# Mixture-of-experts units sized by an ordering of the experts, with 32-token runs computed from the arriving weights

## The chip, the core and the metric

The kernel runs on one core of one Trainium2 chip. The metric is the device time of one execution in microseconds (us), as a median over runs. TensorE is called PE here, VectorE DVE, ScalarE ACT, GpSimd POOL and SyncE SP, as the profile does.

## The reference

Three layers follow each other on 2304 tokens of width 512.

```python
def _attn_ref(q, k, v):                      # (4, 8, 576, 64)
    ...                                      # block-causal attention, blocks of 64
def _moe_ref(x, w_in, w_out):                # 512 -> 2048 -> 512
    h = x @ w_in
    return (h - np.tanh(h)) @ w_out
def _moe2_ref(x, w_skip, w_gate, w1, w2):    # 8 experts, 512 -> 1024 -> 512
    do_compute = x @ w_skip > 0
    out = x.copy()
    xc = x[do_compute]
    e_idx = np.argmax(xc @ w_gate, axis=1)
    gate_w = ...                             # softmax of the logits, at e_idx
    for e in range(8):
        mask = e_idx == e
        y[mask] = gate_w[mask, None] * (np.maximum(xc[mask] @ w1[e], 0.0) @ w2[e])
    out[do_compute] = xc + y
    return out
```

So in the third layer each token that passes the skip gate goes through one expert. With the reference's inputs 1264 of the 2304 tokens do, and experts 0 to 7 get 269, 0, 3, 130, 211, 176, 406 and 69 of them.

## The kernel before, in words

Attention comes first, then the first feed-forward layer (`moe1`, in groups of 384 tokens), then the experts (`Moe2`). The change is in the last part.

While `moe1` finishes a group, it computes that group's gate and scatters for each token a record (row number, gate weight) into the DRAM table `tab` (L685). Each expert has a region of `tab`; unused rows hold a row number past the last token, for which the gather reads zeros and the scatter writes nothing. After four of the six groups, `Route.pick` names the expert with most tokens so far the **lead** (expert 6 here), whose weights are loaded before `moe1` ends. `Route.close` leaves room so that the lead's first 256 rows belong to the first five groups and can be used before the last group is routed.

The experts are computed in **units** of 256 or 128 tokens of one expert. `Moe2.run` walks through **steps** s. A unit of 256 has 8 steps: step z multiplies one 128-wide slice of the hidden layer, `mm1` (L834: 12 matmuls of 256 columns, since each factor is split in a high and a low part), and two steps later `mm2` for that slice (L893: 6 matmuls of 512 columns). A unit of 128 has 4 steps with `mm1_few` (L846, 12 of 256 columns), two transposes (L860) and `mm2_few` (L874, 6 of 512 columns). Before, the units are two of 256 for the lead and seven more from `UNITS` (256, 256, 128, 256, 128, 256, 128), which makes 60 steps. Which expert and rows a unit of `UNITS` gets is computed at run time by `entries` (L1030 to L1092, on DVE) and read into registers by `expert` and `first_row`; an expert of more than 256 tokens takes several units and its weights are loaded for each. If more units are needed, a loop at the end (L1253) computes them one by one; with these inputs it runs zero times.

A unit's weights are 8 pieces of 512 KB. `load_piece` (L769, L772, on SP's queue) brings one into a `stage` buffer, of which there are four; `split_piece` writes its high part (L787, on ACT) and its low part (L788, on DVE) into one of two weight sets. `todo` lists at which step each piece is split; after each split the next load is issued, so four are always on their way. At s = `THEN` the registers are read and the first four loads are issued. A unit's tokens come by `load_rec` (L792) and `gather` (L801, an indirect DMA on POOL), four transposes per 128 tokens (L812) and a split (L819, L820). `finish` (L905, L908) adds the token itself and scatters the result. All instructions stand in each engine's queue in the order in which `run` writes them.

The steps of attention that the prediction compares with are L200 (scores, a full-width fp32 matmul) and L293 (`pv_early`, fp32 matmuls whose result fills 64 of the 128 output partitions, for two heads).

## Time and profile before

| | us |
|---|---|
| median of 3 runs | 868.16 (867.09 to 871.84) |
| the profiled execution, its own time | 870.14 |
| its span, first to last instruction | 868.6 |
| PE busy | 832.7 (96%) |
| DVE busy | 698.7 (80%) |
| ACT busy | 565.6 (65%) |
| POOL busy | 249.3 (29%) |
| DMA, mean rate | 122 GB/s |

Busy time is the time in which an engine had an instruction under way. Matmuls overlap in the pipeline, so a row's mean duration is longer than the distance from one to the next; the distance is read from starts. "Idle before" is time in which an engine had nothing under way, with what ended it behind the arrow. A row of the timeline merges equal instructions that follow each other without a gap: its start, how long the whole row took, and behind the x how many.

### The profile page before, as it was taken

To read this page: it belongs to the slowest core of one execution; us is meant where nothing else is said; L and a number is where in the kernel's file an instruction comes from. 1 tells how busy PE (TensorE), PEld (TensorE's weight loads), DVE (VectorE), ACT (ScalarE), POOL (GpSimd) and SP (SyncE) were. 2 spreads that over 40 slices of the span, in tenths; PEclk is the share of its full clock that TensorE was granted. 3 is DMA by queue.
4 is the path that set the end of the run, shared out by engine and by line. 5 is a ranking of instruction groups with operands and counts; after the bars stand their busy time and mean duration, and the time that the engine had idled before them with its cause. 6 is when DMAs were issued, how large, how long until landed. Compare 5 with 4: busy or idle time off the path is not lost.

```text
span 868.6 us, 14970 instructions
## 1 busy us (share of the span) xinstructions
PE 832.7 (96%) x4715; PEld 710.9 (82%) x4715; DVE 698.7 (80%) x1681; ACT 565.6 (65%) x1332; POOL 249.3 (29%) x314
## 2 busy tenths in 40 slices
PE   7999999999899999999999999999998889999996
PEld 4777777777787989999899898988886789999995
DVE  6899999999799999989986868777797626777772
ACT  5788888888577776776775555646565115565651
POOL 5767777677311111111100010010103221214101
PEclk9899999999999999999999999999999989999998
DMA  7356353652123332232320404222354326687850
GB/s 171 89 143 159 93 141 88 151 127 88 59 80 89 96 121 88 95 122 73 102 89 21 146 11 137 80 68 82 90 191 124 102 103 211 197 299 255 290 193 25
DMA packets 102836, 106.06 MB, mean 122 GB/s; under 512 B 64807, under 2 KB 75175, under 8 KB 102754
## 3 DMA queue, kind: packets, MB, share of 16 engines
q1 hardware_dynamic: 99554, 98.52, 37.8%
q0 software_dynamic: 3200, 6.55, 2.4%
q8 instruction: 38, 0.62, 0.3%
q14 instruction: 44, 0.36, 0.1%
HBM read 82.61 MB, written 23.78 MB: 122 GB/s over the span
## 4 chain that ended last, share of the span: by engine, by line
PE 35%; issue 34%; DVE 17%; ACT 5%; DMA 3%; POOL 3%; SPq 1%; POOLq 0%; DVEq 0%; ACTq 0%
PE h L200 6%; PE h L834 6%; PE acc L893 5%; PE h L508 4%; PE acc L561 4%; DVE w L538 3%; PE acc L266 2%; DVE st L208 2%; DVE w L542 2%; DVE word L51 2%; DVE word L52 1%; DMA xr<-x2s,rec 1%; PE lp L316 1%; PE tp L316 1%; POOL tab L685 1%
## 5 line engine op out<-in xcount | busy, mean ns | idle before, releaser
L508 PE MATMUL h<-xhl,wi 128*128 128x384 f32 x1152 | 220.4, 340 | 1.1 <-DVE xhl L449 1.1
L508 PEld LDWEIGHTS h<-xhl,wi 128*128 128x128 f32 x1152 | 204.9, 188 | 8.8 <-DVE xhl L449 1.3
L561 PE MATMUL acc<-wo,gh 128*128 128x512 f32 x576 | 151.0, 397 | 2.9 <-ACT o L578 2.9
L561 PEld LDWEIGHTS acc<-wo,gh 128*128 128x128 f32 x576 | 105.3, 188 | 21.9 <-ACT o L578 5.0
L240 POOL TENSOR_TENSOR p<-p,st 128x64 f32<-128x64 f32 (+2 forms) x144 | 103.4, 723 | 60.4 <-DVE st L239 27.6
L200 PE MATMUL h<-kT,qbd 128*128 128x128 f32 (+7 forms) x320 | 106.0, 423 | 4.6 <-ACT p L219 1.9
L536 DVE SCALAR_TENSOR_TENSOR w<-h,u 128x384 f32<-128x384 f32 x96 | 53.3, 555 | 46.4 <-ACT t L534 38.9
L561 PE MATMUL acc<-wo,gl 128*128 128x512 f32 x288 | 83.1, 397 | 2.0 <-DVE gl L550 2.0
L685 POOL DMA_INDIRECT tab<-rec,pi x18 | 20.2, 1124 | 212.4 <-DVE pi L683 198.9
L534 ACT ACTIVATE t<-h 128x384 f32<-128x384 f32 x96 | 47.1, 491 | 49.0 <-DVE w L542 49.0
L834 PE MATMUL h<-xhl,wi 128*128 128x256 f32 x576 | 78.7, 286 | 0.0
L533 ACT ACTIVATE u<-h 128x384 f32<-128x384 f32 x96 | 47.2, 492 | 48.2 <-issue 41.1
L834 PEld LDWEIGHTS h<-xhl,wi 128*128 128x128 f32 x576 | 76.0, 192 | 3.2
L893 PE MATMUL acc<-wo,hp 128*128 128x512 f32 x288 | 75.7, 399 | 0.0
L538 DVE SCALAR_TENSOR_TENSOR w<-y,w 128x384 f32<-128x384 f32 x96 | 71.6, 746 | 0.0
L219 ACT ACTIVATE p<-h,st 128x64 f32<-128x64 f32 (+7 forms) x128 | 65.0, 509 | 7.3 <-DVE st L234 5.7
L561 PEld LDWEIGHTS acc<-wo,gl 128*128 128x128 f32 x288 | 53.8, 188 | 16.3 <-DVE gl L550 3.7
L208 DVE TENSOR_REDUCE st<-h 128x1 f32<-128x64 f32 (+7 forms) x128 | 57.0, 445 | 10.3 <-PE h L200 9.5
L200 PEld LDWEIGHTS h<-kT,qbd 128*128 128x128 f32 x320 | 50.6, 196 | 15.9 <-issue 5.8
L881 ACT ACTIVATE hp<-h 128x256 fp32r<-128x256 f32 x48 | 18.4, 384 | 65.1 <-PE h L834 61.2
L542 DVE COPY_PREDICATED w<-k,t 128x384 f32<-128x384 int32 x96 | 57.3, 597 | 3.8 <-ACT k L541 3.7
L541 ACT ACTIVATE k<-u,bias 128x384 f32<-128x384 f32 x96 | 60.0, 625 | 0.0
(233 smaller groups left out, 1611.1 us busy)
## 6 DMA issues: line engine op xcount, KB each, us to landing
stage<-in_moe_w_dram SPq DMA_DIRECT2D x64, 512.0 KB, 4.5
xg<-xTd SPq DMA_DIRECT2D x48, 192.0 KB, 2.4
stage<-in_moe_w_in_dram SPq DMA_DIRECT2D x16, 512.0 KB, 3.8
stage<-in_moe_w_out_dram SPq DMA_DIRECT2D x16, 512.0 KB, 3.2
x2p<-o SPq DMA_DIRECT2D x18, 256.0 KB, 4.4
part<-x2p SPq DMA_DIRECT2D x18, 256.0 KB, 3.0
out_dram<-part SPq DMA_DIRECT2D x18, 256.0 KB, 2.3
x2s<-part SPq DMA_DIRECT2D x18, 256.0 KB, 2.9
```

What stands on the lines that cost most here:

```text
L200: nc.tensor.matmul(s[:, 0:z - a], qb[:, i, :], kT[:, a:z], start=True, stop=True)
L208: nc.vector.reduce_max(nm, ss[0][:, 0:nk], axis=AX.X, negate=True)
L219: nc.scalar.activation(prob[i][:, 0:nk], ss[0][:, 0:nk], AF.Exp, bias=nm, accum_out=st[:, 1, i:i + 1])
L240: nc.gpsimd.tensor_tensor(prob[i][:, 0:nk], prob[i][:, 0:nk], ri.to_broadcast([128, nk]), op=ALU.mult)
L508: nc.tensor.matmul(h[:, 0:TG], w[:, a, c, fs], x[:, b, c], start=(n == 0), stop=(n == 11))
L536: nc.vector.scalar_tensor_tensor(w, h, POLY_C2, u, op0=ALU.mult, op1=ALU.mult)
L538: nc.vector.scalar_tensor_tensor(w, y, POLY_K, w, op0=ALU.add, op1=ALU.mult)
L541: nc.scalar.activation(k, u, AF.Relu, bias=C.bias[:, 1:2])
L542: nc.vector.copy_predicated(w, k.bitcast(I32), t)
L561: nc.tensor.matmul(accs[u][t], g[a][:, t * 128:t * 128 + 128], w[:, b, f], start=(f == 0 and b == 1), stop=(f == NF - 1 and a == 1),)
L834: self.nc.tensor.matmul(h[:, 0:NSLOT], wi[:, a, c, f * 128:f * 128 + 128], x[:, b, c], start=(n == 0), stop=(n == 11))
L893: nc.tensor.matmul(acc[t], hp[:, a, t * 128:t * 128 + 128], wo[:, b, f], start=(f == 0 and b == 1), stop=(f == 7 and a == 1),)
```

## The change

Experts are now put into seven **slots**: slot 0 is the lead, slots 1 to 6 the others by falling token count. Each slot has a capacity, from its units and, for slots 1, 4 and 6, a run of 32 more tokens: 512, 288, 256, 256, 160, 128 and 32. The units stand fixed in the code: 256, 128 and 128 for the lead, 256 each for slots 1 to 3, 128 each for slots 4 and 5; that makes 48 steps. With these inputs every expert fits into its slot, and the loop for what is left over runs zero times again. `Route.close` now leaves 384 rows for the first five groups, so the lead's second unit is gathered early as well.

The runs of 32 tokens are computed by a new function, `few`, without splitting anything: it takes each weight piece in its `stage` buffer as it arrives, in plain fp32. The 32 tokens' rows are read four times over, each time a quarter of the columns, so that one transpose gives all of x. Then each piece of `w1` is multiplied in four matmuls whose results fill 32 output partitions each, 256 columns wide, and each piece of `w2` in eight of 128 columns. `PIECES` is a table by hand that says at which steps the pieces of each slot are used; slot 6 has only a run, so its pieces are not split. Seven sets of weights were loaded after the lead's, now six are. `THEN` is 5 instead of 6, and only the order of the experts has to be known there; the rest of `entries` goes on behind it.

```diff
-THEN = 6
-NSLOT, MORE = 256, 128
-UNITS = (NSLOT, NSLOT, MORE, NSLOT, MORE, NSLOT, MORE)
-NBIG = UNITS.count(NSLOT)
-NENTRY = 20
+THEN = 5
+NSLOT, MORE, FEW = 256, 128, 32
+UNITS = ((NSLOT, 0), (MORE, 0), (MORE, 0), (NSLOT, 1), (NSLOT, 2), (NSLOT, 3), (MORE, 4), (MORE, 5))
+WITH_FEW = (1, 4, 6)
+NSLOTS = 7
+CAP = [sum(n for n, e in UNITS if e == z) + FEW * (z in WITH_FEW) for z in range(NSLOTS)]
+PIECES = {
+    1: (8, 9, 10, 11, 12, 13, 14, 15),
+    6: (18, 18, 19, 19, 21, 21, 22, 22),
+    2: (19, 20, 21, 22, 23, 24, 25, 26),
+    3: (27, 28, 29, 30, 31, 32, 33, 34),
+    4: (35, 36, 37, 38, 39, 40, 41, 42),
+    5: (40, 41, 41, 42, 43, 44, 45, 46),
+}
+NENTRY = 26
+REGION = WROWS + MORE
...
-        v.scalar_tensor_tensor(self.row, self.oh, float(NSLOT), C.base0, op0=ALU.mult, op1=ALU.add)
+        v.scalar_tensor_tensor(self.row, self.oh, float(NSLOT + MORE), C.base0, op0=ALU.mult, op1=ALU.add)
...
-        tp = self.PS("lp")
+        tp = self.PS("h")
...
+        self.recs[1] = self.load_rec(row + NSLOT, self.nc.sync, 1)
...
+    def few(self, row):
+        nc, P = self.nc, self.P
+        rec = P.tile([128, 2], I32, tag="rec3", name="rec3", bufs=2)
+        for g in range(4):
+            nc.gpsimd.dma_start(out=rec[32 * g:32 * g + 32], in_=self.tab[bass.ds(row, FEW), :])
+        yield
+        at = P.tile([128, 1], I32, tag="at3", name="at3", bufs=2)
+        nc.gpsimd.tensor_scalar(at, rec[:, 0:1], 4.0, self.C.quarter[:, 0:1], op0=ALU.mult, op1=ALU.add)
+        xr = P.tile([128, 128], F32, tag="xr3", name="xr3", bufs=2)
+        nc.gpsimd.indirect_dma_start(
+            out=xr, out_offset=None, in_=self.x2s.rearrange("n (q c) -> (n q) c", q=4),
+            in_offset=bass.IndirectOffsetOnAxis(ap=at, axis=0), bounds_check=4 * WROWS + 3, oob_is_err=False,
+        )
+        yield
+        bank = self.PS("lp")
+        nc.tensor.transpose(bank[:, 0:128], xr, self.C.ident)
+        yield
+        xT = self.X.pool.tile([128, TG], F32, tag="xg", name="xT3", bufs=3)[:, 0:128]
+        nc.scalar.copy(xT, bank[:, 0:128])
+        raw = yield
+        quarters = [slice(32 * g, 32 * g + 32) for g in range(4)]
+        for j in range(4):
+            for g, sl in enumerate(quarters):
+                nc.tensor.matmul(
+                    bank[sl, 0:256], xT[:, 32 * j:32 * j + 32], raw[:, 256 * g:256 * g + 256],
+                    start=(j == 0), stop=(j == 3),
+                )
+            if j == 3:
+                hr = self.X.pool.tile([128, TG], F32, tag="xg", name="hr3", bufs=3)[:, 0:256]
+                nc.scalar.activation(hr, bank[:, 0:256], AF.Relu)
+            raw = yield
+        for i in range(2):
+            nc.tensor.transpose(bank[:, 128 * i:128 * i + 128], hr[:, 128 * i:128 * i + 128], self.C.ident)
+        hT = self.X.pool.tile([128, TG], F32, tag="xg", name="hT3", bufs=3)[:, 0:256].rearrange("p (i c) -> p i c", i=2)
+        nc.scalar.copy(hT, bank[:, 0:256].rearrange("p (i c) -> p i c", i=2))
+        for j in range(4):
+            w = raw.rearrange("p (c n) -> p c n", c=2)
+            for c in range(2):
+                for g, sl in enumerate(quarters):
+                    nc.tensor.matmul(
+                        bank[sl, 256:384], hT[:, c, 32 * j:32 * j + 32], w[:, c, 128 * g:128 * g + 128],
+                        start=(j == 0 and c == 0), stop=(j == 3 and c == 1),
+                    )
+            if j < 3:
+                raw = yield
+        o = self.T.tile([128, 512], F32, tag="o", name="o3", bufs=4)[:, 0:128]
+        nc.vector.scalar_tensor_tensor(
+            o, bank[:, 256:384], rec[:, 1:2].bitcast(F32), xr, op0=ALU.mult, op1=ALU.add
+        )
+        self.scattered_one(nc.gpsimd.indirect_dma_start(
+            out=self.out.rearrange("n (q c) -> (n q) c", q=4), out_offset=bass.IndirectOffsetOnAxis(ap=at, axis=0),
+            in_=o, in_offset=None, bounds_check=4 * WROWS - 1, oob_is_err=False,
+        ))
+        yield
+    def run(self, lead, tail, then, experts):
+        K = len(UNITS)
...
-        nt = [n // 128 for n in sizes]
+        nt = [n // 128 for n, _ in UNITS]
+        slot = [e for _, e in UNITS]
+        offset = [sum(UNITS[z][0] for z in range(k) if slot[z] == slot[k]) for k in range(K)]
-        W = [max(k - 1, 0) % 2 for k in range(K)]
-        todo = sorted((at[k] - (5 if nt[k] == 2 else 7) + j, k, j) for k in range(2, K) for j in range(8))
-        loads = iter([(k, j) for _, k, j in todo])
+        todo = sorted((s, e, j) for e in PIECES for j, s in enumerate(PIECES[e]))
+        loads = iter([(e, j) for _, e, j in todo])
...
-                recs[1] = self.load_rec(lead[1] + NSLOT, self.nc.sync)
+                recs[2] = self.load_rec(lead + offset[2], self.nc.sync, 1)
...
             if s == THEN:
-                assert next(after, None) is None
-                where.update(enumerate(units(), 2))
+                where.update(enumerate(experts(), 1))
                 for _ in range(4):
                     load_next()
...
-            for n, c in [(n, c) for n, c in tps if s == at[n] + c - 4]:
+            for n, c in [(n, c) for n, c in tps if s == at[n] + c - 3]:
                 self.split_x(tps.pop((n, c)), xx[n], c)
...
+            for e in WITH_FEW:
+                t = PIECES[e][0]
+                if s == max(t - 6, THEN):
+                    fews[e] = self.few(where[e][1] + sum(n for n, x in UNITS if x == e))
+                    next(fews[e])
+                if s in (t - 3, t - 2, t - 1):
+                    next(fews[e])
             while todo and todo[0][0] <= s:
-                _, n, j = todo.pop(0)
-                self.split_piece(raws.pop((n, j)), W[n], j)
+                _, e, j = todo.pop(0)
+                raw = raws.pop((e, j))
+                if e in slot:
+                    self.split_piece(raw, e % 2, j)
+                if e in fews:
+                    fews[e].send(raw)
                 load_next()
             for n in range(1, K):
-                if n > 1 and s == max(at[n] - 12, THEN):
-                    recs[n] = self.load_rec(where[n][1], nt=nt[n])
-                if s == (at[n] - 8 if n > 1 else 4):
+                if slot[n] and s == max(at[n] - 10, THEN):
+                    recs[n] = self.load_rec(where[slot[n]][1], nt=nt[n])
+                if s == at[n] - 6:
                     xrs[n] = self.gather(recs[n], n, nt[n])
-                if s == (at[n] - 5 if n > 1 else 6):
+                if s == at[n] - 4:
                     xx[n] = self.new_x(n)
-                if n == 1 and s == 6:
-                    for c in range(2):
-                        self.split_x(self.transposes(xrs[n], c, ("tp", "h")[c]), xx[n], c)
-                if n > 1 and 0 <= s - at[n] + 5 < nt[n]:
-                    tps[n, s - at[n] + 5] = self.transposes(xrs[n], s - at[n] + 5, ("tp", "h")[s - at[n] + 5])
+                if 0 <= s - at[n] + 4 < nt[n]:
+                    tps[n, s - at[n] + 4] = self.transposes(xrs[n], s - at[n] + 4, ("tp", "h")[s - at[n] + 4])
...
+    meta = {}
+    def experts():
+        for z in range(NSLOTS - 1):
+            e = expert(meta["order"][0:1, z:z + 1], [SP, POOL])
+            yield e, e * REGION
+    m2.run(lead[0] * REGION, tail, lambda: entries(nc, cp, d, C, route, meta), experts)
+    runs = meta["runs"]
+    total = nc.values_load(runs[0:1, 2, 0:1], min_val=0, max_val=NENTRY - 1,
+                           skip_runtime_bounds_check_because="so many runs hold every token")
+    with tc.If(total > 0):
+        with tc.For_i(0, total, 1) as j:
+            e = expert(runs[0:1, 0, bass.ds(j, 1)], [SP])
+            r = first_row(runs[0:1, 1, bass.ds(j, 1)], [POOL])
             m2.one(e, r)
     xp.close()```

In `entries` the first eight DVE operations now give the experts' order, and only then the rest follows. `tab` grows with `REGION`, and some constants are made once at the start.

**On POOL, behind the last group's scatters into `tab`** (`xr` is gathered tokens, `rec` a unit's records, `stage` is not on this engine). Before:

```order
L685 DMA tab<-rec,pi 20736x2 x3
L801 DMA xr<-x2s,rec_8283 128x512 x2
L1208 TENSOR_LOAD meta x7
L792 ISA
L792 DMA rec_8539<-tab 128x2x2
L801 DMA xr<-x2s,rec_8539 128x512 x2
```

Now:

```order
L705 DMA tab<-rec,pi 21888x2 x3
L821 DMA xr<-x2s,rec_8087 128x512
L1288 TENSOR_LOAD order x6
L963 ISA
L963 DMA rec_8495<-tab 32x2
...
L966 TENSOR_SCALAR at_8500<-rec_8495,quarter 128x1
L968 DMA xr_8502<-x2s,at_8500 128x128
L821 DMA xr<-x2s,rec_8296 128x512
L812 ISA
L812 DMA rec_8534<-tab 128x2x2
```

The lead's second gather stands ahead of the register loads as before, but for 128 tokens; then come four small record loads (the middle ones left out) and the gather of the first run, and only behind it the gather of the lead's third unit.

**On PE, steps 6 to 8** (a step is `mm1` and then an older step's `mm2`). Before:

```order
L834 MATMUL h<-xhl,wi_107 128x256 x12
L893 MATMUL acc<-wo_108,hp 128x512 x6
L812 MATMUL tp<-ident,xr 128x128 x4
L812 MATMUL h<-ident,xr 128x128 x4
L834 MATMUL h<-xhl,wi_107 128x256 x12
L893 MATMUL acc<-wo_108,hp 128x512 x6
```

Now:

```order
L854 MATMUL h<-xhl,wi_110 128x256 x12
L913 MATMUL acc<-wo_111,hp 128x512 x6
L974 MATMUL lp<-ident,xr_8502 128x128
L854 MATMUL h<-xhl,wi_110 128x256 x12
L913 MATMUL acc<-wo_111,hp 128x512 x6
L866 MATMUL h<-wi_110,xhl 128x256 x12
L913 MATMUL acc<-wo_111,hp 128x512 x6
L982 MATMUL lp<-stage,xT_8558 32x256 x4
L832 MATMUL tp<-ident,xr 128x128 x4
```

Where PE transposed the lead's second unit behind step 6, it now transposes the first run's tokens (L974); a step and a half later the first piece's matmuls follow (L982).

**On PE, steps 18 to 22**, where the pieces of slot 6 go by two in a step. Now:

```order
L913 MATMUL acc<-wo_3402,hp 128x512 x6
L982 MATMUL lp<-stage,xT_8976 32x256 x8
L854 MATMUL h<-xhl,wi_3401 128x256 x12
L913 MATMUL acc<-wo_3402,hp 128x512 x6
L832 MATMUL tp<-ident,xr 128x128 x4
L854 MATMUL h<-xhl,wi_3401 128x256 x12
L913 MATMUL acc<-wo_3402,hp 128x512 x6
L991 MATMUL lp<-ident,hr_9057 128x128 x2
L998 MATMUL lp<-stage,hT_9122 32x128 x16
```

Before, no matmul read a `stage` buffer; now L982 and L998 stand in PE's queue, and what is behind them waits until a piece has landed. L998 follows right behind the transposes (L991) whose copy by ACT it needs.

## Rows read from the trace of the kernel before

**Rows 1.** Busy time by stretch (PE, PEld, DVE, ACT, POOL; then PEclk, DMA share, GB/s).

```profile
673.85:860.26 186.41, 181.24 (x1167) 163.81 (x1165) 119.31 (x201) 86.19 (x142) 39.87 (x37) 0.98 0.60 193
691.58:703.19 11.61, 6.61 (x27) 5.82 (x26) 1.81 (x3) 1.56 (x3) 2.69 (x3) 0.71 0.69 207
773.00:791.00 18.00, 18.00 (x123) 16.45 (x122) 14.18 (x19) 11.45 (x21) 4.13 (x4) 1.00 0.86 287
```

**Rows 2.** Groups of PE instructions by shape (count | busy us, mean ns | idle before).

```profile
L834 PE MATMUL h<-xhl,wi 128*128 128x256 f32 x576 | 78.7, 286 | 0.0
...
L846 PE MATMUL h<-wi,xhl 128*128 128x256 f32 x144 | 19.3, 283 | 0.0
```

**Rows 3.** Timeline of PE, steps of a 256-unit (start us, us).

```profile
708.82 1.60 PE L834 MATMUL h<-xhl,wi 128*128 128x256 f32 x12
...
711.65 1.59 PE L834 MATMUL h<-xhl,wi 128*128 128x256 f32 x12
...
714.48 0.60 PE L812 MATMUL tp<-ident,xr 128*128 128x128 f32 x4
714.83 1.68 PE L834 MATMUL h<-xhl,wi 128*128 128x256 f32 x12
```

**Rows 4.** Timeline of PE, steps of a 128-unit and the last matmuls.

```profile
850.99 1.57 PE L846 MATMUL h<-wi,xhl 128*128 128x256 f32 x12
...
854.00 1.59 PE L846 MATMUL h<-wi,xhl 128*128 128x256 f32 x12
...
857.27 2.99 PE L874 MATMUL acc<-wo,hp 128*128 128x512 f32 x12
```

**Rows 5.** Timeline of PE, steps 6 to 8.

```profile
691.58 0.60 PE L812 MATMUL tp<-ident,xr 128*128 128x128 f32 x4
697.18 1.12 PE L812 MATMUL h<-ident,xr 128*128 128x128 f32 x4 [5.00 <-DMA xr<-x2s,rec]
697.95 2.91 PE L834 MATMUL h<-xhl,wi 128*128 128x256 f32 x12
...
703.19 1.59 PE L834 MATMUL h<-xhl,wi 128*128 128x256 f32 x12
```

**Rows 6.** Timeline of POOL over the same stretch.

```profile
679.85 0.98 POOL L685 DMA_INDIRECT tab<-rec,pi  x1 [0.30 <-issue]
687.64 1.05 POOL L801 DMA_INDIRECT xr<-x2s,rec  x1 [6.81 <-PE h L834]
689.00 1.02 POOL L801 DMA_INDIRECT xr<-x2s,rec  x1 [0.31 <-issue]
691.44 0.77 POOL L792 DMA_DIRECT2D rec<-tab  x1 [1.42 <-issue]
699.18 1.05 POOL L801 DMA_INDIRECT xr<-x2s,rec  x1 [6.96 <-DMA rec<-tab]
```

**Rows 7.** Timeline of SP's queue over the same stretch.

```profile
683.80 0.39 SPq L792 DMA_DIRECT2D rec<-tab  x1
688.90 1.91 SPq L769 DMA_DIRECT2D stage<-in_moe_w_dram  x4
```

**Rows 8.** Groups of full-width fp32 matmuls in attention, by shape.

```profile
L200 PE MATMUL h<-kT,qbd 128*128 128x512 f32 x32 | 16.5, 597 | 0.0
...
L200 PE MATMUL h<-kT,qbd 128*128 128x128 f32 x64 | 12.5, 281 | 1.3 <-ACT qbd L135 1.3
```

**Rows 9.** Timeline of PE, one pass of the 64-wide fp32 matmuls.

```profile
111.89 0.88 PE L293 MATMUL lp<-pt,vr 128*64 128x256 f32 x8
112.69 0.33 PE L255 MATMUL acc<-ident,p 128*128 128x128 f32 x1
```

**Rows 10.** Groups in the expert part: work per weight piece and per hidden copy.

```profile
L788 DVE TENSOR_TENSOR wo<-stage,wo 128x1024 fp32r<-128x1024 f32 x28 | 34.3, 1224 | 11.7 <-ACT wo L787 11.6
...
L787 ACT CAST wi<-stage 128x1024 fp32r<-128x1024 f32 x28 | 29.5, 1055 | 6.0 <-DMA stage<-in_moe_w_dram 6.0
...
L865 ACT CAST hp<-lp 128x256 fp32r<-128x256 f32 x12 | 4.4, 368 | 1.0 <-PE lp L860 1.0
```

**Rows 11.** DMA issues in the expert part: the weight pieces (KB, us to landing).

```profile
stage<-in_moe_w_dram SPq DMA_DIRECT2D x56, 512.0 KB, 4.5
```

More of the change, by code (lines that the diff above doesn't have):

```diff
@@ L487, in __init__ @@
         nc.vector.tensor_tensor(self.before, self.col, self.entry[:, 0:e, 0:e], op=ALU.is_lt)
+        self.quarter = t([128, 1], F32, name="quarter")
+        for z in range(4):
+            nc.gpsimd.memset(self.quarter[32 * z:32 * z + 32], float(z))
         self.thr = index("thr", [e, d.NT // MORE], [[0, e], [MORE, d.NT // MORE]])
@@ L911, in finish, with scattered_one @@
             )
-            for prev in self.scattered:
-                self.tc.declare_no_dep(ins.ins, prev.ins, reason="each token has a row of its own")
-            self.scattered.append(ins)
+            self.scattered_one(ins)
+    def scattered_one(self, ins):
+        for prev in self.scattered:
+            self.tc.declare_no_dep(ins.ins, prev.ins, reason="each token has a row of its own")
+        self.scattered.append(ins)
     def new_x(self, k=0):
@@ L929, in prepare @@
             self.split_x(self.transposes(self.xrs[0], c, ("tp", "h")[c]), self.xx[0], c)
-    def run(self, sizes, lead, tail, then, units):
-        K = len(sizes)
+    def few(self, row):
[52 more added lines that the diff above has]
+        yield
```

120 lines of the change are left out of this document (52 added, 68 removed).

## The prediction

> **What bounds the kernel now.** I first read busy time by stretch, for the expert part alone: of its 186.4 us PE is busy for 181.2, at the full clock of 2.4 GHz nearly all the time (0.98); DVE has 119, ACT 86, and the DMA engines are used to 60% [rows 1]. So the time there is the number of matmuls times their distance. The groups count 576 and 144 matmuls of the first product, 12 to a step: 60 steps, and no unit beyond the nine planned [rows 2]. The timeline gives the price of a step: one of a 256-unit takes 711.65 - 708.82 = 2.83 us; with the four transposes of 128 new tokens it takes 714.83 - 711.65 = 3.18, so these cost 0.35 [rows 3]. A step of a 128-unit takes 3.01, 0.18 more, for its two transposes [rows 4]. Last, the one place where PE stands: behind the first half of the lead's second gather it waits 5.00 us for the other half, and the next step runs at half clock (697.95 to 703.19) [rows 5]. Over that stretch the granted clock is 0.71, against 1.00 in the dense one; it fell to 1.2 GHz after PE had stood idle [rows 1].
>
> **Steps removed.** With the reference's inputs all experts fit their slots (269 into 288, 211, 176 into 256 each, 130 into 160, 69 into 128, 3 into 32; the lead's 406 into 512), so 60 steps become 48 and nothing is left for the loop. One 256-unit goes: 8 x 2.83 + 2 x 0.35 = 23.3 us. One 128-unit goes: 4 x 3.01 + 0.35 = 12.4. The lead's second 256-unit becomes two of 128, the same matmuls with transposes: 8 x 0.18 = 1.4 more. Together **-34.3 us**, all on PE's own path [rows 3, 4]. The end, two matmul groups, one addition, a scatter, is the same [rows 4].
>
> **The stall at the start: moved, not removed.** The lead's second unit is now gathered right behind the last scatters, whose issue ends at 680.8 on POOL, and PE wants it two steps later: no wait. But POOL's next work is the first run: four record loads, one wait for all, a gather, and PE wants that at 691.58, behind step 6, where it stood before. Record loads can't start before the scatters have landed, which SP's queue dates to 683.80 [rows 7]; a load takes POOL 0.77 us and about 0.3 between, so the fourth is out at about 688 [rows 6]. SP meanwhile has one short record load and then six registers to read, and needs no whole `entries`, so the four weight loads go out some 2.3 us earlier than at 688.90 [rows 7], at 686.6, in the middle of these. The row to compare with is POOL's record load at 691.44: issued behind the four weight loads, it had not landed until 699.18 less the issue, over 6.9 us later [rows 6]. Just so the half gather issued at 689.00 among them landed at 697.1 [rows 5, 6]. So I let the records land with the weights, at 686.6 + 8.2 = 694.8, and the gather take 1 us to issue and 2.5 to land: PE goes on at 698.3 instead of 697.2, and once more at half clock for a step. At the other bound the records get ahead of the weights and nothing is waited for: -5.0 for the wait, -2.4 for the slow step (5.24 against 2.83), -1.1 for the one just added. I take **+1**, since both transfers that were issued near the weights came late; range -7.4 to +3. Queued behind the waiting POOL is the gather for the lead's third unit; it goes out at once after, some 7 us before PE reaches it.
>
> **The runs of 32.** Their matmuls are fp32. The trace holds such a matmul as two records (L293: 128 for the 64 that the order shows). From 128 to 512 columns a record grows from 281 to 597 ns: 0.823 ns a column and 176 ns fixed, which overlaps [rows 8]. A piece of `w1` is four matmuls of 256 columns, a piece of `w2` eight of 128: both 2 x 1024 columns, 1.69 us one after the other. Whether they run one after the other is the large unknown. Nearest are the attention's 64-wide ones: eight records, four of 256 and four of 128 columns, for two halves of the array. One after the other they would take 1536 x 0.823 = 1.26 us; from the first start to the next matmul's it took 0.80 [rows 9]. So the two halves ran side by side (0.63), with 0.17 for going in and out. I take four quarters side by side, because two cost no more than one; a piece is then 0.42, and 24 pieces 10.1. The bounds are two at a time, +10.1, and one at a time, +30.3. The Trainium skill (TensorEngine Tiling (Array Packing), Performance Considerations) says that up to 32 columns of the stationary operand give four column tiles; no row here shows four, and by that rule the sum keeps 10.1 where by the row alone it would have 20.2.
>
> The pieces come in 8, 4 and 8 separate runs, 20 x 0.17 = 3.4. Three transposes each, 9 x 0.09 = 0.8. And L998 stands right behind L991: PE waits there for ACT's copy, 0.37, behind the cast of the same piece, 1.06, which ACT takes while PE still has `mm2` [rows 10]: I take 1.0 each, 3.0 (bounds 0.5 and 1.5). Together **+17.3**. ACT's three small copies and DVE's one addition per run lie beside PE; DVE had 67 us free.
>
> **Weights in time.** PE now reads `stage` itself and so waits for landings. A piece takes 4.5 us to land [rows 11], and dense loads reach 287 GB/s [rows 1]. In steps 18 to 22 twelve pieces are wanted, four are there, so 8 x 0.52 MB = 4.2 MB in 14.6 us; PE needs about 15.5 for these steps. The buffer of a run's piece is given back only when PE has read it, one step before the next is wanted: I take 2.5 (bounds 0 and 12). In steps 40 to 42 seven pieces are split, three in one step: 3.7 us of DVE and 3.2 of ACT [rows 10], beside the last addition of slot 3; the hidden copies come late by about one step, which the distance of two hides but for about 1. Together **+3.5**. Fewer loads in all (48 pieces for 56) gain nothing by themselves: before, PE never waited for one.
>
> The constants, the wider table and the shorter `entries` are a few small operations beside PE: 0; if `entries` were still to be waited for, that is in the stall's range.
>
> **Sum:** -34.3 + 1 + 17.3 + 3.5 = -12.5 us. Against the profiled execution, 870.1 (span 868.6), that is 857.6. The median of the runs, 868.2, lies 2.0 lower, so I forecast **855.7**.
>
> **The rivals.** A difference of 0.5%, 4.3 us, is about what a measurement can tell from no change.
> - *The quarters run one after the other* (the slower one): nothing in the trace runs four at once. Then the runs cost 30.3 more: 886. It decides once they overlap less than some 1.8-fold (40.4 over 10.1 + 12.5), where the gain is used up; the pair in rows 9 speaks against it. Two at a time: 866.
> - *The stall goes:* the four record loads are tiny and the first is out before any weight; if all land ahead, 8.4 less: 847. Against it stand the two late transfers.
> - *PE starves on the pieces:* if the loads among gathers and scatters reach half the rate, the twelve pieces take 14 us longer and cost 12 instead of 2.5: 865. Before, at 287 GB/s, PE did not stand, but it also never waited for a piece directly.
> - *The array drains at each change of width.* In rows 9 a change in and out costs 0.17 us; if each of the 40 edges waited out the fixed 176 ns of a record [rows 8], they would cost 7.0 instead of 3.4: 859. The Trainium skill (TensorEngine Tiling, Key Properties) states that changing the tiling mode drains TensorE; by the row the edge is half of that.
> - *The change doesn't do what it says:* an expert over its slot would be computed in the loop at the end; with these inputs none is.
>
> **The numbers.** Forecast 0.53, own range 849 to 863; stall gone 0.14; drain 0.08; starving 0.12; two at a time 0.06; one at a time 0.07. Below 863.8 lie the forecast but for 0.03, the stall, the drain and 0.04 of starving: faster 0.76. Up to 872.5 the rest of these and the two at a time: same 0.17. Slower 0.07. The range 845 to 867 leaves out the slow case, part of the two-at-a-time case and the best of the stall case, some 0.15.
>
> **What would show it.** PE's groups: 384 `mm1` matmuls in the 256-wide form, 192 in the other. The four records of a quarter set start within 0.1 us of each other, and a piece takes 0.4 to 0.6 us, not 1.7. The timeline has one wait on the first run's gather between 691 and 699 and half clock behind it; waits of about 1 us on ACT's copy three times; small waits on `stage` in steps 18 to 22. Wrong would be pieces that take over 1 us each, PE idle over 10 us on `stage`, or a final loop that runs.

## The result

The changed kernel takes 859.0 us (median of 4 runs, 855.96 to 861.16) where the kernel before, on the same chip, takes 868.5 (4 runs): a ratio of 0.9883, interval 0.9839 to 0.9926. The profiled execution took 861.16 us with a span of 859.4; before, 870.1 and 868.6. From the dense part up to `finish`, a line of the kernel after is one of before plus 20; in edited kernels it lies a few further on.

First the expert part, from the first expert matmul to the last, and the place of the stall (busy time by stretch: PE, PEld, DVE, ACT, POOL; then PEclk, DMA share, GB/s; these answer to [rows 1]), and PE's groups in the expert part by shape, which answer to [rows 2]:

```profile
678.08:850.02 171.94, 163.51 (x1244) 136.27 (x1242) 91.77 (x164) 68.11 (x124) 45.21 (x50) 1.00 0.57 179
692.53:702.50 9.97, 8.19 (x55) 7.31 (x56) 1.54 (x3) 1.38 (x4) 3.21 (x4) 1.00 0.68 245
```

```profile
L854 PE MATMUL h<-xhl,wi 128*128 128x256 f32 x384 | 52.5, 286 | 0.0
...
L866 PE MATMUL h<-wi,xhl 128*128 128x256 f32 x192 | 26.9, 289 | 0.9 <-DVE wi L808 0.9
...
L998 PE MATMUL lp<-stage,hT 128*32 128x128 f32 x192 | 7.6, 279 | 2.2 <-ACT hT L993 1.5 <-DMA stage<-in_moe_w_dram 0.6
L982 PE MATMUL lp<-stage,xT 128*32 128x256 f32 x96 | 7.4, 390 | 0.0
...
L832 PE MATMUL tp<-ident,xr 128*128 128x128 f32 x28 | 4.5, 284 | 3.4 <-DMA xr<-x2s,rec 3.4
```

The part takes 171.94 us for 186.41, 14.5 less. It holds (384 + 192) / 12 = 48 steps, as planned; a record takes 286 and 289 ns, for 286 and 283 [rows 2]; the loop at the end doesn't run. A step without a run costs what it did, 2.82 us in a unit of 256 and 3.02 in one of 128 (timeline of PE, steps 26 and 46, counted from 0):

```profile
771.95 1.59 PE L854 MATMUL h<-xhl,wi 128*128 128x256 f32 x12
...
774.77 1.59 PE L854 MATMUL h<-xhl,wi 128*128 128x256 f32 x12
...
840.81 1.60 PE L866 MATMUL h<-wi,xhl 128*128 128x256 f32 x12
...
843.83 1.59 PE L866 MATMUL h<-wi,xhl 128*128 128x256 f32 x12
```

PE stands idle more than before: 8.4 us of the part for 5.2. But the part begins 4.2 us later (678.08 for 673.85), and the span ends 9.4 us after PE's last matmul where it was 8.3. So 14.5 - 4.2 - 1.1 = 9.2 is what the span lost.

The timeline of PE in two steps with a piece of the first run of 32 (start us, us) shows the new cost:

```profile
707.46 1.68 PE L866 MATMUL h<-wi,xhl 128*128 128x256 f32 x12
...
710.68 0.64 PE L982 MATMUL lp<-stage,xT 128*32 128x256 f32 x8
711.25 1.70 PE L866 MATMUL h<-wi,xhl 128*128 128x256 f32 x12
```

Eight records of 390 ns in the mean, 3.1 us one after the other, lie in 0.64: the quarters overlap. The step takes 711.25 - 707.46 = 3.79 us against 3.01 without a piece [rows 4]: a lone piece costs **0.78**, not 0.42 + 0.17 = 0.59.

The timeline of PE, POOL and SP's queue at the start of the experts answers to [rows 5 to 7]:

```profile
692.53 0.66 PE L832 MATMUL tp<-ident,xr 128*128 128x128 f32 x4 [2.21 <-DMA xr<-x2s,rec]
...
700.60 0.30 PE L974 MATMUL lp<-ident,xr 128*128 128x128 f32 x1 [1.78 <-DMA xr<-x2s,at]
```

```profile
685.35 1.05 POOL L821 DMA_INDIRECT xr<-x2s,rec  x1 [0.30 <-issue]
689.71 2.27 POOL L963 DMA_DIRECT2D rec<-tab  x4 [3.31 <-DMA tab<-rec,pi]
693.39 0.26 POOL L966 TENSOR_SCALAR at<-rec,quarter 128x1 int32<-128x1 int32 x1 [1.40 <-DMA rec<-tab]
```

```profile
691.98 2.04 SPq L789 DMA_DIRECT2D stage<-in_moe_w_dram  x4
```

The four record loads go out in 2.27 us and are all issued before the first weight load at 691.98; they have landed by 693.39. PE waits 2.21 for the gather of the lead's second unit and 1.78 for the first run's, 4.0 in all, at full clock, where it waited 5.00 and then ran a step at half clock [rows 1, 5].

Later in the part, in steps 21, 22, 28 and 44, stand these waits (timeline of PE):

```profile
756.94 1.13 PE L998 MATMUL lp<-stage,hT 128*32 128x128 f32 x32 [0.56 <-ACT hT L993]
...
762.81 0.65 PE L998 MATMUL lp<-stage,hT 128*32 128x128 f32 x16 [0.65 <-DMA stage<-in_moe_w_dram]
...
781.75 0.66 PE L832 MATMUL tp<-ident,xr 128*128 128x128 f32 x4 [1.19 <-DMA xr<-x2s,rec]
...
835.82 0.50 PE L866 MATMUL h<-wi,xhl 128*128 128x256 f32 x2 [0.87 <-DVE wi L808]
```

The late begin shows ahead of the part: PE waits for the dense part's last additions, and these for the partial sums, whose loads stand on SP's queue behind the lead's record loads (timelines of PE and of SP's queue):

```profile
669.48 1.32 PE L622 MATMUL h<-ident,part 128*128 128x128 f32 x8 [1.94 <-DVE part L604]
```

```profile
664.85 0.93 SPq L812 DMA_DIRECT2D rec<-tab  x2
665.89 1.31 SPq L722 DMA_DIRECT2D part<-x2p  x3
```

### The profile page after: what moved, and what is told of

Same layout as the page of the kernel before. It is cut to its first block, busy times and chain, and to the rows that moved or that the text cites. A ratio compares the mean times of both kernels' runs of the same rounds, so it can differ in the third digit from the quotient of the medians.

```text
span 859.4 us, 15080 instructions
## 1 busy us (share of the span) xinstructions
PE 819.6 (95%) x4792; PEld 685.8 (80%) x4792; DVE 672.9 (78%) x1643; ACT 547.0 (64%) x1314; POOL 253.3 (29%) x338
## 5 line engine op out<-in xcount | busy, mean ns | idle before, releaser
L528 PE MATMUL h<-xhl,wi 128*128 128x384 f32 x1152 | 220.2, 340 | 1.1 <-DVE xhl L468 1.1
L528 PEld LDWEIGHTS h<-xhl,wi 128*128 128x128 f32 x1152 | 205.5, 189 | 8.7 <-DVE xhl L468 1.3
L200 PE MATMUL h<-kT,qbd 128*128 128x128 f32 (+7 forms) x320 | 107.5, 429 | 2.6 <-ACT qbd L135 1.3
L705 POOL DMA_INDIRECT tab<-rec,pi x18 | 18.5, 1026 | 213.7 <-DVE pi L703 198.8
L554 ACT ACTIVATE t<-h 128x384 f32<-128x384 f32 x96 | 47.1, 491 | 49.3 <-DVE w L562 49.2
L581 PEld LDWEIGHTS acc<-wo,gl 128*128 128x128 f32 x288 | 53.8, 188 | 16.5 <-DVE gl L570 3.9
L200 PEld LDWEIGHTS h<-kT,qbd 128*128 128x128 f32 x320 | 51.3, 198 | 14.3 <-issue 6.2
L555 ACT ACTIVATE y<-u,bias 128x384 f32<-128x384 f32 x96 | 59.1, 616 | 0.0
L901 ACT ACTIVATE hp<-h 128x256 fp32r<-128x256 f32 x32 | 12.3, 384 | 66.5 <-PE h L854 60.4
L54 POOL TENSOR_TENSOR wo<-word,wo 128x512 fp32r<-128x512 f32 x16 | 21.0, 1312 | 110.4 <-ACT wo L53 110.4
L570 DVE TENSOR_TENSOR gl<-w,gh 128x384 fp32r<-128x384 f32 x96 | 52.7, 549 | 0.0
## 6 DMA issues: line engine op xcount, KB each, us to landing
stage<-in_moe_w_dram SPq DMA_DIRECT2D x56, 512.0 KB, 4.3
stage<-in_moe_w_in_dram SPq DMA_DIRECT2D x16, 512.0 KB, 4.2
stage<-in_moe_w_out_dram SPq DMA_DIRECT2D x16, 512.0 KB, 3.5
```

Of the source, the lines that this page charges most:

```text
L200: nc.tensor.matmul(s[:, 0:z - a], qb[:, i, :], kT[:, a:z], start=True, stop=True)
L528: nc.tensor.matmul(h[:, 0:TG], w[:, a, c, fs], x[:, b, c], start=(n == 0), stop=(n == 11))
L555: nc.scalar.activation(y, u, AF.Square, bias=C.bias[:, 0:1])
L570: nc.vector.tensor_tensor(gl, w, gh.bitcast(F32), op=ALU.subtract)
L581: nc.tensor.matmul(accs[u][t], g[a][:, t * 128:t * 128 + 128], w[:, b, f], start=(f == 0 and b == 1), stop=(f == NF - 1 and a == 1),)
```

## The experiments

In each group the runs share a chip and the runs of before (869.8, 869.6 and 870.0 us in the three groups). "After the last hidden matmul" counts from the start of the dense part's last record of L528 (L508 before).

**The change once more.**

> The changed kernel once more, unaltered. Theory A (mine): in the first profile the change gained 14.5 us inside the expert part (186.4 to 171.9 us) and lost 4.2 ahead of it by chance: a late landing of the scatters held SP's queue, PE stood 1.9 us and its clock fell. Then the expert part takes 171 to 173 us again, and its start lies anywhere between 674 and 679 us; the median over more runs is 855 to 859. Theory B: the extra record load ahead of the part loads on SP's queue delays the start each time: expert start at 677 or later again, median 858 to 860.

860.21 us (858.88 to 861.22), ratio 0.9889 (0.9869 to 0.9908). The experts start 19.6 us after the last hidden matmul, 19.9 in the first profile; in the one of before it was 16.8. This time PE waits 3.66 us for the gather of the lead's second unit, a step at half clock follows (5.18 us for 2.82), and the first run's gather is then in time. The part takes 174.1 us, not the 171 to 173 of Theory A, it begins at 675.7, not at B's 677 or later, and the median lies just above the range of B. The price of the start varies between executions; the rest repeats (0.72 for 1.19 at the gather in step 28, 0.88 for 0.87 at the split in step 44).

**Full width for four quarters.**

```diff
-            for g, sl in enumerate(quarters):
-                nc.tensor.matmul(bank[sl, 0:256], xT[:, 32 * j:32 * j + 32], raw[:, 256 * g:256 * g + 256], ...)
+            nc.tensor.matmul(bank[:, 0:256], xT, raw[:, 0:256], start=(j == 0), stop=(j == 3))
```

(and likewise for the pieces of `w2`; this leaves out three quarters of the products.)

> Left out: three quarters of the arithmetic of the runs of 32. The four (or eight) 32-wide fp32 matmuls of a piece become one (or two) full-width ones with as many columns (256, and 128 twice), so the stream is 0.42 us a piece as before, and what remains different is the width. In the changed kernel a piece costs 0.79 us where it stands alone in a step. Theory A, the change of the array's width costs about 0.37 a run of pieces: the piece falls to about 0.45 and the kernel is 6 to 7 us faster than the changed one. Theory B, what costs is any fp32 matmul between the others: the piece stays at 0.7 to 0.8, the time within 1 us.

858.81 us (856.81 to 860.22), ratio 0.9882 (0.9858 to 0.9905). Two steps of PE's timeline:

```profile
709.78 1.79 PE L866 MATMUL h<-wi,xhl 128*128 128x256 f32 x12
...
713.00 0.59 PE L981 MATMUL lp<-stage,xT 128*128 128x256 f32 x2
713.24 1.78 PE L866 MATMUL h<-wi,xhl 128*128 128x256 f32 x12
```

The step takes 3.46, so a piece of as many columns in the stream costs 0.45 where no width changes, and 0.78 where it does. Going in and out of the narrow form thus costs 0.33. The 6 to 7 us of Theory A did not come: the median is 1.4 lower, with intervals that overlap, and the profiled execution 4.1. Against the second profile of the change, steps 8 to 15 took 29.8 us for 32.1 and steps 35 to 42 28.2 for 30.7, but steps 16 to 23 31.0 for 31.1 and steps 24 to 34 33.6 for 32.9: there waits for stages and for a gather took the gain back.

**One strip for all four quarters.**

```diff
-                    bank[sl, 0:256], xT[...], raw[...], start=(j == 0), stop=(j == 3),
+                    bank[0:32, 0:256], xT[...], raw[...], start=(j == 0 and g == 0), stop=(j == 3 and g == 3),
```

(and a second transpose for each run, which fills the rest of the bank.)

> Left out: the first products of the runs of 32 all go to one quarter of the array and are summed there, instead of side by side in four (the second products are unaltered). Theory A, four quarters run at once in the changed kernel: a piece of w1 grows from 0.64 us (its row) to about 1.9, and 12 pieces cost 15 us more. Theory B, they run two at a time or one after the other already: 7.5 or 0 us more.

874.8 us, in a single execution. PE's timeline has a piece of `w1` as

```profile
710.76 1.91 PE L983 MATMUL lp<-stage,xT 128*32 128x256 f32 x8
```

1.91 for 0.64 with the same eight records: 1.27 more for each of 12 pieces, 15.2, and the time is 14.6 up. In the changed kernel all four run at once.

**Record loads on POOL's queue.**

```diff
-        self.recs, self.xrs, self.xx = {0: self.load_rec(row, self.nc.sync)}, {}, {}
+        self.recs, self.xrs, self.xx = {0: self.load_rec(row)}, {}, {}
```

(and the same for the second unit's; the lead's number is then read on POOL too.)

> The records of the lead's first two units are loaded on POOL's queue instead of SP's, so that the loads of the last group's parts on SP don't stand behind a wait for the scatters. Theory A (start delayed by chance through this queue): DVE no longer waits for the parts, expert start at 673 to 675 us in the profile, median 0 to 3 us under the changed kernel's. Theory B (the start is late for another reason): expert start still at 677 or later, time unaltered.

863.56 us (861.83 to 865.8), ratio 0.993 (0.9903 to 0.9956): 3.4 slower than the change, which neither theory had. The partial sums came early and PE hardly waited for them (0.32); it waited 4.10 for the gather instead, and the experts started 21.5 us after the last hidden matmul. So what sets the start is the chain of scatters landing, record load, gather. The record load went out 9.6 us after the last hidden matmul, for 6.6 and 7.4, since the scatters landed later still; the run with the late weight load comes back to this.

**The kernel before, a second profile.**

> The kernel before, unaltered, for a second profile of its start of the experts. In the first one the first matmul of the experts stands 16.8 us after the start of the last hidden matmul of the dense part; in the four profiles of the changed kernel with its own order of loads it stands 18.8 to 19.9 us after it. Theory A, the change makes the start later by 2 to 3 us (record load of the lead unit later, part loads behind it): here 16 to 17.5 us again, and the record load is issued 4.5 to 5.5 us after the last hidden matmul. Theory B, the start varies from one execution to the next whatever the kernel: here 18 us or more.

869.04 us. The record load is issued 4.96 us after the last hidden matmul (5.07 in the first profile; 6.64 and 7.40 in two of the change), as Theory A said; the experts start 18.2 us after it, as B said, with a granted clock of 0.79 from 668 to 676 where the first profile had 1.00. So a later record load belongs to the change, and on top of it the clock makes the start vary by more than 1 us in either kernel.

**Partial sums ahead of the records.**

```diff
-PREP = 8
+PREP = 9
```

> The lead unit's record loads are issued one step later on the SP queue, behind the three loads of the partial sums and not ahead of them. Theory A, the start of the experts hangs on the chain scatter landing, record load, gather: the wait of TensorE for the partial sums (1.9 to 2.3 us) goes, but the record load is issued some 1.5 us later and the gather with it, so TensorE waits for the gather instead: 859 to 862 us, no better than 860.2. Theory B, the wait for the partial sums and the half clock behind it cost what the start lost: 2 to 3 us less, 857 to 858 us.

858.21 us (855.98 to 858.31), ratio 0.9861 (0.9839 to 0.9883). The wait for the partial sums shrinks from 2.25 to 0.32, the record load is issued 8.47 us after the last hidden matmul, the experts start 18.2 us after it, for 19.6. The time is near Theory B's, but the next two kernels, whose loads stand as in the change, start theirs 18.1 and 18.5 us after it, and the interval overlaps that of the change: not settled.

**Two pieces at a time.**

```diff
-        for j in range(4):
-            for g, sl in enumerate(quarters):
+        held = []
+        for j in range(4):
+            held.append((j, raw))
+            if j % 2:
+                for jj, r in held:
+                    for g, sl in enumerate(quarters):
...
```

> A run of 32 takes its weight pieces two at a time (a pair shares one stretch of narrow matmuls), and the turning of its hidden values and the copy stand a step ahead of the first w2 pair. The same products; 24 stretches of narrow matmuls become 12. Theory A, each stretch costs 0.33 us at its two edges and each wait for the copy of the hidden values some 0.6 us, on TensorE's path: 12 x 0.33 + 3 x 0.6 = 5.8 us less, 854.4 us, a step with a lone pair about 4.3 us and not twice 3.8. Theory B, the time between the runs is bounded by weights and gathers that arrive no earlier: the freed time returns as waits for the stage and the gather, and only the stretches of steps 9 to 16 gain (4 x 0.33 + 0.6 = 1.9 us), 858.3 us. As the full-width run gave back 1.4 of 6, I lean to B with 857 to 859.

856.46 us (855.87 to 857.88), ratio 0.9853 (0.9835 to 0.9871), 3.7 less than the change: between the two. A step behind a pair and a step with a pair, from PE's timeline (the last row is cut off by the view's end):

```profile
708.35 1.69 PE L866 MATMUL h<-wi,xhl 128*128 128x256 f32 x12
...
711.49 1.60 PE L866 MATMUL h<-wi,xhl 128*128 128x256 f32 x12
...
714.63 1.07 PE L986 MATMUL lp<-stage,xT 128*32 128x256 f32 x16
715.63 0.62 PE L866 MATMUL h<-wi,xhl 128*128 128x256 f32 x3
```

The step with the pair takes 4.14, 1.13 more than one without [rows 4], and the one behind a pair 711.49 - 708.35 = 3.14, another 0.13 more. So a pair costs 1.26, a second piece in the same stretch 1.26 - 0.78 = 0.48, and going in and out 0.78 - 0.48 = 0.30, near the 0.33 above. The expectation counts twelve stretches fewer; but the pieces of slot 6 stood two to a step already, so the 20 stretches of the change become 12. Eight at 0.33 and two waits of 0.46 for ACT's copy, in steps 12 and 39, which are gone, make 3.6, while waits for stages in steps 21 and 22 grow from 0.65 to 1.5 (0.60, 0.27 and 0.61). The 3.7 agree with that within the spread of the runs, 2.0 us: the price in Theory A holds, its count does not.

**Pairs, and the gather of the third normal expert's unit a step earlier.**

```diff
-                if s == at[n] - 6:
+                if s == at[n] - (7 if n == 5 else 6):
```

> As the kernel with pairs, and the gather of the third normal expert's unit is issued one step (3.6 us) earlier, seven steps ahead of its first matmul. Theory A, the wait of 0.7 to 1.4 us for that gather before its transposes is on the path: it goes, 1 us less than with the pairs alone. Theory B, what follows is bounded by the arrival of weights: no difference within 0.5 us. Against: the gather then stands ahead of a scatter of results in POOL's queue, which holds nobody up.

855.24 us (854.19 to 857.79), ratio 0.9844 (0.9822 to 0.9865). The wait goes from 0.85 to 0.54 only, and the 1.2 us between the two medians lie within their spread: not settled.

**The last weight load of the lead behind the record loads.**

```diff
-            if 0 <= n < 8:
+            if 0 <= n < 7:
                 raws[n] = m2.load_piece(lead[0], n)
+            if n == 9:
+                raws[7] = m2.load_piece(lead[0], 7)
...
+        m2.split_piece(raws.pop(7), 0, 7)
```

> The last of the eight weight loads of the lead expert is issued behind the record loads and the loads of the partial sums, and its split into high and low parts behind the lead unit's first transposes; no load then shares the DMA queues with the last three scatters of the table of records. In all seven profiles of the changed kernel the record load of the lead unit is issued 6.6 to 9.6 us after the last hidden matmul, 5.7 us or more behind the end of the third scatter; in both profiles of the kernel before 5.0 us after it, 2.5 behind the end of the scatter, and there the last load's data moved ahead of the scatters. Theory A, that load holds up the landing of the scatters: the record load is issued 3 to 5 us after the last hidden matmul, the wait for the partial sums goes, the experts start 2 us earlier, 858 us. Theory B, the scatters land late for another reason: the record load stays at 6.5 to 7.5 us, the time at 860 +- 1; or the late split of the last piece costs ACT and DVE 1 us each at the start of the experts and it becomes slower, 861 to 862.

The mechanism shows. The first and the third of the last three scatters on POOL's timeline, and SP's queue beside them, in the second profile of before:

```profile
653.27 1.71 POOL L685 DMA_INDIRECT tab<-rec,pi  x1 [33.04 <-DVE pi L683]
...
656.68 1.78 POOL L685 DMA_INDIRECT tab<-rec,pi  x1 [0.30 <-issue]
```

```profile
654.16 0.37 SPq L772 DMA_DIRECT2D stage<-in_moe_w_dram  x1
660.95 0.37 SPq L792 DMA_DIRECT2D rec<-tab  x1
```

The second and the third in the change, and SP's queue:

```profile
656.79 0.98 POOL L705 DMA_INDIRECT tab<-rec,pi  x1 [0.31 <-issue]
658.07 0.98 POOL L705 DMA_INDIRECT tab<-rec,pi  x1 [0.30 <-issue]
```

```profile
656.79 0.37 SPq L792 DMA_DIRECT2D stage<-in_moe_w_dram  x1
```

The third in this run, and SP's queue:

```profile
656.12 0.98 POOL L705 DMA_INDIRECT tab<-rec,pi  x1 [0.30 <-issue]
```

```profile
659.86 0.93 SPq L812 DMA_DIRECT2D rec<-tab  x2
660.90 1.31 SPq L722 DMA_DIRECT2D part<-x2p  x3
662.48 0.39 SPq L792 DMA_DIRECT2D stage<-in_moe_w_dram  x1
```

And the DMA issues of 650 to 672 us in the change (KB each, median us from issue to landing), then this run:

```profile
stage<-in_moe_w_dram SPq DMA_DIRECT2D x1, 512.0 KB, 6.9
...
tab<-rec,pi POOLq DMA_INDIRECT x3, 6.8
```

```profile
tab<-rec,pi POOLq DMA_INDIRECT x3, 3.7
```

From the end of the third scatter to the record load it is 660.95 - 658.46 = 2.5 us before, 664.85 - 659.05 = 5.8 in the change and 659.86 - 657.10 = 2.8 here. Before, the load is issued during the first scatter and lands in 3.8 us, the scatters in 4.2; in the change it is issued with the second scatter, and both take 6.8 or more. With the load out of the way the scatters land in 3.7, and the experts start 15.9 us after the last hidden matmul. Two runs above have the same effect more strongly: where the loads of the partial sums go out beside the scatters too, these take 7.8 us (partial sums ahead of the records) and 8.3 (record loads on POOL's queue), and those loads themselves 7.4 and 7.9 for 2.8 in the change:

```profile
tab<-rec,pi POOLq DMA_INDIRECT x3, 7.8
```

```profile
tab<-rec,pi POOLq DMA_INDIRECT x3, 8.3
```

But the time is 861.28 us (859.5 to 863.74), ratio 0.9909 (0.9884 to 0.9934), no better than the change. In its profile 3.7 us are gained at the start; PE then waits 3.02 for the gather of the lead's second unit, the step behind it takes 4.44 for 2.82, and in step 22 PE waits 2.0 for stages. Waits of that kind stood in the second profile of the change too (3.66, then 5.18 for a step); what is new against it is 0.6 us in the first step and 2.3 in steps 21 to 23. So the gain was in part given back to what comes next; and since the profiled execution, 859.5, is the fastest of the four, what made the median is not in it.

**The gather of the lead's second unit right behind the first's.**

```diff
         self.xrs[0] = self.gather(self.recs[0])
+        self.xrs[1] = self.gather(self.recs[1], nt=1)
```

(its later issue goes, and gathers of 128 and of 256 tokens get buffers of their own.)

> The gather of the second unit of the lead expert is issued right behind that of the first, before the last group's scatters, some 15 us earlier. Theory A, TensorE's wait before that unit's transposes (2.2 to 3.7 us, in the fifth step) and the half clock behind it are on the path: the wait goes, 3 us less, 857.2 us. Theory B, the next thing is late too: the first run of 32 (record loads and gather, known to TensorE only when the order of experts is) takes it over, its wait grows from 0.7 to 1.8 us to 3.5 to 5, and the time stays at 859.5 to 860.5. I lean to B, since its gather is issued after the order of experts is known, whatever TensorE does.

860.9 us (860.47 to 863.83), ratio 0.9893 (0.9872 to 0.9915). That wait is gone, and PE's timeline has in its stead

```profile
700.11 0.30 PE L977 MATMUL lp<-ident,xr 128*128 128x128 f32 x1 [4.74 <-DMA xr<-x2s,at]
```

The time and the longer wait are Theory B's, but its reason is not what the trace shows (timelines of POOL and of SP's queue):

```profile
683.06 0.98 POOL L705 DMA_INDIRECT tab<-rec,pi  x1 [0.30 <-DVE eup L1151]
689.86 2.29 POOL L966 DMA_DIRECT2D rec<-tab  x4 [5.82 <-PE tp L834]
695.30 0.26 POOL L969 TENSOR_SCALAR at<-rec,quarter 128x1 int32<-128x1 int32 x1 [3.15 <-DMA rec<-tab]
```

```profile
691.63 2.04 SPq L789 DMA_DIRECT2D stage<-in_moe_w_dram  x4
```

POOL had read the order of the experts by 684.7. The record loads of the first run go out 5.8 us behind the last scatter, 5.0 of which pass until the scatters have landed (SP's own record load, released by that landing, goes out at 689.08). The fourth of them then goes out together with the first weight load and lands in 3.5 us, the median in 1.8, so POOL waits 3.15 for the records where it waited 1.40 in the change. That is what the prediction had assumed for the change, though with 8.2 us.

**These together.** Pairs, both earlier gathers, and the first run's pieces in steps 10 to 15:

```diff
-    1: (8, 9, 10, 11, 12, 13, 14, 15),
+    1: (10, 11, 12, 13, 14, 14, 15, 15),
```

> Pairs of pieces, the earlier gather of the third normal expert's unit, the earlier gather of the lead expert's second unit, and the first run of 32 two steps later (its eight pieces in steps 10 to 15 and not 8 to 15), so that its gather has two more steps to land. Theory A, the waits at the start of the experts come from gathers alone: of the 3.6 us of waits in the steps 4 to 6 in the kernel with pairs and early gather, and 1.5 us of steps at half clock behind them, 3 to 5 go: 850.5 to 852 us. Theory B, the weights bound it: the last pieces of the first run are two to a step and the loads start later, so waits for the stage in steps 14 to 22 give back 2 us or more: 853 to 855.

855.04 us (851.89 to 856.68), ratio 0.9825 (0.9799 to 0.985), the same as pairs and the first early gather alone, 855.24. The waits in the first steps of the experts went from 3.6 to 1.88 us, but the median shows nothing of it; the figure is Theory B's, but not its reason: waits for stages in steps 14 to 22 come to 0.8 (0.15, 0.33 and 0.31), for 0.7 in the kernel with pairs and the early gather. What the profile shows instead is a wait of 0.89 for ACT's copy in step 14, where the first pair of `w2` now stands right behind the transposes that it needs, and 0.65 more in step 44.

> As the one before, with the last weight load of the lead expert issued behind the record loads too. If that load holds up the scatters (Theory A of the run that does this alone): 2 us less than the one before, 848.5 to 850. If not, or if the late split costs as much: the same within 1 us.

851.65 us (848.6 to 853.42), ratio 0.9774 (0.9752 to 0.9797): 3.4 less than the one before, where 2 were expected, and the fastest of all. The record load is issued 3.82 us after the last hidden matmul, for 7.00. The late load, worth nothing alone, pays in this kernel; which of its other edits made room for it was not separated.

## Why the prediction was right, and where it was not

The forecast of 855.7 lies 3.3 below the result. The sum, against the first profile:

- **Steps removed, -34.3: right.** 48 steps at 2.82 and 3.01 us, 0.35 for new tokens. PE bounded the part before, and the steps that are left cost what they did, so each that went took its full price with it.
- **Four quarters at once: right, and shown** by the run with one strip. The Trainium skill's statement (TensorEngine Tiling (Array Packing), Performance Considerations), that up to 32 columns give four tiles, is borne out: 0.64 us for 1.91.
- **Runs of 32, +17.3: too small.** By difference they cost 171.94 - (186.41 - 34.3) + 3.4 - 1.5 - 1.2 = 20.5, where 3.4 is what the start gained and 1.5 and 1.2 are the waits below. Added up from measured prices they are 24 x 0.45 + 20 x 0.33 + 0.8 + 1.5 = 19.7. The term that failed is "20 x 0.17 = 3.4": a stretch costs 0.30 to 0.33 for going in and out, 6.0 to 6.6 in all. The price 0.17 came from two halves of 64 columns [rows 9] and did not carry over to four quarters of 32. The stream, 0.45 to 0.48 a piece for the 0.42 taken, was nearly right. The rival of the array that drains at each change had the edge right (7.0 / 20 = 0.35 for in and out), and its rule in the Trainium skill (TensorEngine Tiling (Array Packing), Key Properties) goes with what the runs show; that the array drains is one reading of the 0.33, which no run here separates from another start-up cost of the narrow form. The waits on ACT's copy were three of about 0.5, not 1.0: 1.5 for 3.0.
- **The stall, +1: the mechanism half wrong.** I let the records land with the weight loads. Both came later than I had them, since both wait for the last scatters, whose issue ended at 685.05 and not at 680.8. But the four record loads went out in 2.27 us where I had some 4, and so they were out when the first weight load went, at 691.98. PE waits 1.78 instead of 6.7. It hung on half a microsecond: the fourth was issued at 691.5; in the run with the gather of the lead's second unit issued early the fourth was issued at 691.7, with the first weight load, landed in 3.5 us, and PE waited 4.74. And the gather of the lead's second unit, "no wait", came late by 2.21: its own issue ended at 686.4, and PE went on 6 us later. In all about -3.4 (4.0 of waits for 5.0 and 2.4 at half clock). In the second profiles of both kernels it was 3.66 of waits and 2.36 at half clock, for 0.85 + 3.81 and 1.08 before: 6.0 for 5.7, near no change. So the gain of 3.4 is that of one execution.
- **Weights in time, +3.5: right in kind, less in size.** 0.65 in step 22, and 0.87 in step 44, where PE stood for the split of the last expert's `w1`, whose cast had waited for its stage; 1.5 together.
- **Not in the sum: the gather of the third normal expert's unit, +1.2.** It is issued six steps ahead where it was eight, behind the scatters of results on POOL; its second half was issued at 777.39, and PE went on at 781.75, 4.4 us later. This should have been read from the diff: each gather of a normal unit moved by two steps and its transposes by one, so it has two steps to land where it had three.
- **Not in the sum: the start of the experts, +4.2, and the end, +1.1.** I took the dense part's tail for unchanged. Of the 4.2, 1.1 had passed before the last hidden matmul; in the second profiles that matmul stands at 656.0 and 656.1, so that part is no price of the change. From there on the change costs 3.1 in the first profiles and 1.4 in the second (19.6 for 18.2). The record load goes out 1.6 to 2.4 us later after the last hidden matmul, because the last three scatters land while a weight load's packets are moving; the runs with that load moved show it. Why scatters and load stand in another order than before, though neither's code was changed, can be followed one step back: the load goes out when DVE has split the piece before (L788, now L808), and that split starts 0.36 us ahead of the first scatter in both profiles of before and 0.01 ahead in both of the change, behind 0.27 of idle time that the profile puts down to an activation (L554). Why DVE waits there stays open. So does the 1 us at the end: POOL's last scatter ends 7.3 us before the span does, for 6.3. It is no chance, for PE's last matmul ends 8.3 us before the span in both profiles of before and 9.4 in both of the change.

So the total came near by errors of opposite sign, and that they cancel is in part luck. In the first profiles the runs (3.2), the gather (1.2), the late start (4.2) and the end (1.1) cost 9.7 more than forecast, the stall (4.4) and the waits for weights (2.0) 6.4 less; 9.7 - 6.4 is the 3.3 that the forecast was low. It comes out even because the runs are taken as what the other terms leave. In the second profiles the part takes 174.1 us for 185.0, 10.9 less, and the start loses 1.6 and the end 1.1: 8.3, nearly the same total from other terms.

## What to carry to other kernels

Price a new kind of instruction by its transitions as well as its stream, and put pieces of it together: two at a time gave 3.7 us of the 20. When a table moves gathers nearer to their use, hold each issue against the landing time of the rows, 4 to 7 us here, as carefully as the matmuls. And a chain of scatter, record load and gather at a boundary is worth a look at what shares the DMA queues with it; but a link made faster pays only when the next is not late already.

## What was not expected

- Three scatters of a few bytes per row land in 3.7 us with no load beside them, in 6.8 when a 512 KB load is issued with the second, and in 7.8 and 8.3 when three loads of 256 KB go out beside them too; the 512 KB load takes 6.9, against 4.5 for the median of the expert part before [rows 11]. The Trainium skill (DMA: Bandwidth & Descriptors, Latency and other measured facts) says that the fixed cost of a DMA lies mostly in the round trip to the memory and falls with a lighter load on it; the direction agrees, the 3 us are more than it gives for that.
- A matmul with 32 columns of stationary operand takes the time of a full one (390 ns a record for 383), four at once, but 0.30 to 0.33 us more each time the width changes and back.
- The same program starts its experts 1.4 us apart (16.8 and 18.2 us after the last hidden matmul in the kernel before), by where the granted clock falls from 2.4 to 1.2 GHz after PE has stood.
